# Starting the x w_val products earlier in the attention loop: two w_val tiles loaded and decoded two steps sooner, three column tiles open at once

## The chip, the core and the metric

The kernel runs on one core of a Trainium2 chip. The metric is the device time of one execution in microseconds, lower is better. Engines are named as the profile names them: PE (TensorE matmul; PEld is its weight load), DVE (VectorE), ACT (ScalarE), POOL (GpSimd), SP (the engine whose queue issues the loads).

## The reference, cut to what matters

```
for each chunk c of 32 tokens, every batch and head:                  # attention over a local window
    k_full = [mem_k (8 keys), k[c_start-16 : c_end+8]]                # the same for v
    a = softmax(q_c @ k_full.T / 8);   attn[c] = a @ v_full
x = attn as (1536 tokens, 512)
val = x @ w_val;   gate = sigmoid(x @ w_gate)                         # 512 x 1536 weights
x = (gate * val) @ w_out
out = sum over 4 experts e of  p[:, e] * (relu(x @ w1[e]) @ w2[e])    # p: normalized domain_probs
```

`w_gate`, `w_val` and `w_out` arrive as 64-bit numbers; the kernel decodes them itself.

## The kernel before

**The attention loop.** The tokens form 4 blocks of 384, the heads 4 pairs; a *unit* is one pair in one block, 16 units in all, block by block. The loop over `i` (0 to 16) runs *step* i, and in each step three units are in work: the queries and keys of unit i+1 are multiplied (`S`, 24 + 6 matmuls), the exponentials of unit i are transposed on PE (`T`), copied out on ACT (`C`), and multiplied by the values of unit i-1 (`O`), whose normalized result is transposed too (`X`). What X leaves in PSUM is split into a high part `xs` on ACT (`H`, line 1034) and a low part on DVE (`L`, line 1038): together they are rows of x, 128 columns of one block.

**The order is written by hand.** Each engine executes its instructions in the order in which the program names them. `FIRST`, `STEP0` (steps 0 to 4) and `STEP` (later steps) are strings of letters that give this order: `O{h} S{j} T{i} Q{q} R{r} a{h} r{h} N{h} m{j} M{j} s{j} W{w} C{i} F{fa} X{h} W{w2} b{t} A{t} H{h} c{t} E{j} L{h} F{fb} D{t}` with h = i-1, j = i+1. Besides those above: `a r N` are DVE's normalization, `m M s` mask, maximum and scaling of the maximum (DVE, line 972 the last), `E` the six exponentials on ACT, `Q` the loads of the unit four ahead, `R` raw weight tiles up to a number, `W` warm-up matmuls on zeros (line 933), `F` a number of products of x and w_val ("fills").

**Decoding a weight tile.** `b A c D` decode one raw tile: `b` shifts the low word (DVE, line 136), `A` rescales the high word (ACT, line 142), `c` joins them (DVE, line 146), and `D` makes the high part (ACT, line 160) and the low part (POOL, line 161). `TICKS` says in which steps this is done, `AHEAD` how many raw tiles are to be loaded by each step; the ring of raw tiles has four buffers.

**The products.** One *fill* is one product of a 128 x 128 piece of w_val with 384 tokens of x, written (f, k) below: column tile f of w_val, and rows k, which are the columns of x that unit k of the block made. It takes three matmuls: line 181 (high, high), line 182 (w high, x low) and line 183 (w low, x high). Four of them, k = 0 to 3, fill a tile in PSUM (`pv`), which ACT copies out (line 1053). The pool of these tiles has three buffers; the warm-ups write into one more tile of the same pool. `FILLS` says how many fills each step takes; up to step 3 all of them stand at the end of the step, from step 4 on half of them (`fa`) before T and X. The list `todo` gives their order.

**After the loop** PE goes on with the rest of x w_val, the gate, w_out and the experts, until the end of the span.

Of the kernel before, what the change touches and what calls it, by code (L numbers as in the profile page):

```python
# [38 lines left out]
RAWS = 4  # L39
# [13 lines left out]

VW = NG * NC * (D + 1)
KQ = VW + KC
TICKS = (0, 0, 1, 1, 1, 1, 1, 1, 1, 1, 1, 1, 1, 1)
FILLS = (0, 0, 0, 2, 3, 4, 4, 4, 4, 9, 9, 9, 9, 9, 10, 10, 10)
AHEAD = (1, 2, 3, 4, 5, 6, 7, 8, 9, 10, 11, 12)
WARM = (2, 2, 2, 2, 0)
WARM_2 = (1, 1, 1, 0, 0)  # L60

FIRST = "W10 S0 m0 M0 s0 Q3 E0 W5"
N0 = 5
STEP0 = (
    "O{h} S{j} T{i} Q{q} R{r} a{h} r{h} N{h} m{j} M{j} s{j} W{w} C{i} F{fa} X{h} W{w2} b{t} A{t} H{h} c{t} E{j} L{h} "
# [7 lines left out]
def fused_kernel(ctx: ExitStack, tc: tile.TileContext, kq0, kq1, kvw, kvc, vl, w_g, w_v, w_o, w_1, w_2, probs, out):  # L73
# [6 lines left out]
    def ps_tile(name):  # L80
        pool = banks[0]
        if banks[1] is not None:
            pool = banks[n_ps[0] % 8 >= 3]
            n_ps[0] += 1
        return pool.tile([128, 512], F32, tag="m", name=name)
# [23 lines left out]
    def raw_to(n):  # L109
        while len(raws) < min(n, n_64):  # L110
            i = len(raws)
            r = rawp.tile([128, 1024], U32, tag="raw", name=f"raw{i}")
            nc.sync.dma_start(out=r, in_=src[order[i][0]][order[i][1]].bitcast(U32))
            raws.append(r)
# [35 lines left out]
    def split_now(tp, n):  # L150

        up, down = raw_parts(n)
        t2 = low_bits(tp, n, down)
        yield
        t1 = high_bits(tp, n, up)
        yield
        joined(t1, t2)
        yield
        w = w_tile(wp, order[n])
        nc.scalar.copy(out=w[:, 0], in_=t1)  # L160
        nc.gpsimd.tensor_tensor(out=w[:, 1], in0=t1, in1=f32(w[:, 0]), op=ALU.subtract)  # L161
# [23 lines left out]
    def bt(blk):  # L185
        return slice(blk * BT, (blk + 1) * BT)
# [706 lines left out]
    with tc.tile_pool(name="gp1", bufs=NV) as gp1:  # L893
        begun = [0]
# [15 lines left out]
        def load(m):  # L910

            if m >= n_u + 2:
                return
            kv, n = kv_b[m % 3], keys(m)
            if m == 0:
                nc.sync.dma_start(out=kv[:, KQ - KB:KQ + BT + KB], in_=kq0)
                return
            for h in range(2):
                c = KQ - n if h == 0 else KQ
                if m == 1:  # L920
                    src, c1 = kq1[h], c + n + BT
                elif m < n_u:
                    src = kvw[m - 2, h] if m < N_ONCE else kvc[m - N_ONCE, h]
                    c, c1 = c - (VW if h == 0 else 0), c + n + BT + (VW if h else 0)
                else:
                    src, c = vl[m - n_u, h], c - VW if h == 0 else c + BT + n
                    c1 = c + VW
                nc.sync.dma_start(out=kv[h::2, c:c1], in_=src)

        def warm_up(n):  # L930

            for _ in range(n):
                nc.tensor.matmul(out=ps_w[:, :BT], lhsT=zero[:, :128], rhs=zero, start=True, stop=True)
# [106 lines left out]
        def proj(ps, key, t, k):  # L1040
            w, x = W[key], x_t[k]
            c = slice(k * 128, (k + 1) * 128)
            mm3(ps[:, :t.stop - t.start], w[:, 0, c], w[:, 1, c], x[:, 0, t], x[:, 1, t], k == 0, k == KD - 1)

        def v_part(blk, steps):

            pss = {}
            for f, k in steps:
                if k == 0:
                    pss[f] = ps_tile(f"pv{f}_{blk}")  # L1050
                proj(pss[f], ("v", f), bt(blk), k)
                if k == KD - 1:
                    nc.scalar.copy(out=g_t[f][:, bt(blk)], in_=pss.pop(f)[:, :BT])
                yield
# [15 lines left out]
        def g_tile(pool, f):  # L1070
            g_t[f] = pool.tile([128, B * S], F32, tag="g", name=f"g{f}")

        with tc.tile_pool(name="ps_s", bufs=2, space=PSUM) as ps_s, \
                tc.tile_pool(name="ps_t", bufs=2, space=PSUM) as ps_t, \
                tc.tile_pool(name="ps_x", bufs=1, space=PSUM) as ps_o, \
                tc.tile_pool(name="att", bufs=1) as att:
            kv_b = [att.tile([128, 2 * KQ + BT], F32, name=f"kv{i}") for i in range(3)]
            zero = att.tile([128, BT], mybir.dt.bfloat16, name="zero")
            nc.vector.memset(zero, 0.0)

            def clear(eng, i, c0, c1):
                eng.memset(kv_b[i][:, c0:c1], 0.0)

            R0, KL = KQ + BT, KC - KB
            load(0)
            clear(nc.vector, 1, KQ - KB, KQ)
            clear(nc.vector, 1, R0, R0 + KB)
            clear(nc.gpsimd, 2, KL, KQ)
            clear(nc.vector, 2, R0, R0 + KB + VW)
            load(1)  # L1090
            load(2)
            clear(nc.vector, 0, KL, KL + VW)
            clear(nc.gpsimd, 0, R0 + KB, R0 + KB + VW)
            make_identity(nc, ident)
            clear(nc.gpsimd, 1, KL, KL + VW)
            clear(nc.gpsimd, 1, R0 + KB, R0 + KB + VW)
            for i in range(3):
                clear(nc.vector, i, 0, KL)
                clear(nc.vector, i, R0 + KB + VW, R0 + KQ)
            warm = tp.tile([128, 1], F32, tag="warm", bufs=1, name="warm")  # L1100
            nc.scalar.activation(out=warm, in_=ident[:, 0:1], func=AF.Exp)
            nc.gpsimd.dma_start(out=p_in, in_=probs)
            for f in range(NV):
                g_tile(gp1, f)

            def parts(blk, fs):
                steps = [(f, k) for f in fs for k in range(KD)]
                return [v_part(blk, steps)] * len(steps)

            todo = [v_part(0, [(0, 0), (0, 1), (0, 2), (1, 0), (1, 1), (1, 2), (0, 3), (1, 3)])] * 8  # L1110
            todo += parts(0, range(2, 6)) + parts(1, range(4)) + parts(0, [6]) + parts(1, range(4, 7)) + parts(0, [7])
            todo += parts(1, [7]) + parts(2, range(NV))
            at = [0]

            def fill_to(n):
                while at[0] < min(n, len(todo)):
                    next(todo[at[0]])
                    at[0] += 1

            tk = []  # L1120
            parts_of = dict(S=scores, m=mask, M=max_, s=neg_max, E=exps, T=turn, C=turned, O=values, a=sums, r=inverse,
                            N=normal, X=put_x, H=x_hi, L=x_lo)

            def run(ops):

                for op in ops.split():
                    what, i = op[0], int(op[1:])
                    if what in parts_of:
                        if 0 <= i < n_u:
                            parts_of[what](i)  # L1130
                    elif what == "Q":
                        load(i)
                    elif what == "R":
                        raw_to(i)
                    elif what == "b" and i:
                        tk.append(split_now(tp, begun[0]))
                        begun[0] += 1
                        next(tk[0], None)
                    elif what in "Ac" and i:
                        next(tk[0], None)  # L1140
                    elif what == "D" and i:
                        next(tk.pop(), None)
                    elif what == "F":
                        fill_to(at[0] + i)
                    elif what == "W":
                        warm_up(i)

            ps_w = ps_tile("warm")
            run(FIRST)
            for i in range(n_u + 1):  # L1150
                n = FILLS[i]
                run((STEP0 if i < N0 else STEP).format(
                    h=i - 1, i=i, j=i + 1, q=i + 4, t=TICKS[i] if i < len(TICKS) else 0, fa=n // 2 if i > 3 else 0,
                    fb=n - n // 2 if i > 3 else n, r=AHEAD[i] if i < len(AHEAD) else begun[0] + RAWS - 1,
                    w=WARM[i] if i < len(WARM) else 0, w2=WARM_2[i] if i < len(WARM_2) else 0))
            fill_to(len(todo))
            for gen in todo:
                for _ in gen:
                    pass
            nc.vector.reduce_sum(out=p_sum, in_=p_in, axis=AX.X)  # L1160
            nc.vector.tensor_scalar(out=p_sum, in0=p_sum, scalar1=1e-9, scalar2=None, op0=ALU.add)
            nc.vector.reciprocal(out=p_sum, in_=p_sum)
            nc.vector.tensor_tensor(out=p_sb, in0=p_in, in1=p_sum.to_broadcast([128, NT, NE]), op=ALU.mult)
        with tc.tile_pool(name="gp2", bufs=KF - NV) as gp2, \
# [30 lines left out]
            for c in range(NCT):  # L1195
# [3 lines left out]
                for f in range(KF):  # L1199
                    i = c * KF + f  # L1200
# [119 lines left out]
```

## Time and profile before

| | us |
|---|---|
| median of 3 runs (lowest to highest) | 841.86 (841.25 to 843.28) |
| the profiled execution: its own time | 843.08 |
| the profiled execution: span of the program in the trace | 841.3 |
| PE busy in the span | 834.4 (99%) |
| DVE, ACT, POOL busy | 513.6, 392.0, 84.7 |

The profile is that of one execution. A busy PE is not a PE at its peak: matmuls are pipelined, a recorded matmul overlaps the next one, and the distance from one start to the next is what it costs.

### The profile page before, as it was taken

The numbers are of one execution on the slowest core, as the hardware profiler recorded it, in microseconds if no ns is written. First come the engines' busy times: TensorE is split into PE (matmuls) and PEld (weight loads), VectorE is DVE, ScalarE is ACT, GpSimd is POOL, SyncE is SP. The second block draws the span as 40 slices with busy tenths as digits, with TensorE's granted clock in tenths as the row PEclk, the third lists the DMA queues.
The fourth block names the chain that finished last, engine by engine and source line by source line (L and its number), as shares of the span: only waits on it lengthen the run. The fifth ranks groups of instructions, "written<-read, shape, count | busy, mean of one in ns | idle before, by whom it ended". The sixth has DMA issues, their size and how long they took to land.

```text
span 841.3 us, 13728 instructions
## 1 busy us (share of the span) xinstructions
PE 834.4 (99%) x5246; PEld 756.6 (90%) x5246; DVE 513.6 (61%) x966; ACT 392.0 (47%) x832; POOL 84.7 (10%) x98
## 2 busy tenths in 40 slices
PE   9999999999999999999999999999999999999997
PEld 6899998888888888889989989989999999999997
DVE  6754246432342229387988788788757557646747
ACT  4865355332232335435345345346355445545542
POOL 2321000000000000000000000000001343243231
PEclk9999999999999999999999999999999999999999
DMA  7976043211210001595887887731697999999983
GB/s 273 378 263 205 2 151 121 79 51 51 76 61 15 0 1 76 213 322 209 336 307 261 340 308 256 296 129 51 229 349 222 256 298 330 297 276 303 336 184 95
DMA packets 63058, 168.32 MB, mean 200 GB/s; under 512 B 6656, under 2 KB 28560, under 8 KB 62992
## 3 DMA queue, kind: packets, MB, share of 16 engines
q1 hardware_dynamic: 52160, 157.59, 52.4%
q0 software_dynamic: 10832, 9.86, 7.6%
q8 instruction: 41, 0.67, 0.3%
q14 instruction: 25, 0.20, 0.1%
HBM read 103.06 MB, written 54.53 MB: 187 GB/s over the span
## 4 chain that ended last, share of the span: by engine, by line
PE 98%; ACT 1%; DMA 0%; DVE 0%; POOL 0%; issue 0%; ACTq 0%
PE b L181 5%; PE d L182 5%; PE d L183 5%; PE b L182 5%; PE b L183 5%; PE d L181 5%; PE pv L181 4%; PE pv L183 4%; PE pv L182 4%; PE pg L182 4%; PE pb L182 4%; PE pb L181 4%; PE pg L183 4%; PE pg L181 4%; PE pb L183 4%; PE B L183 3%
## 5 line engine op out<-in xcount | busy, mean ns | idle before, releaser
L530 POOL DMA_DIRECT2D acc<-st x57 | 49.3, 950 | 673.7 <-DVE st L528 673.2
L181 PE MATMUL b<-yo,w 128*128 128x384 f32 x256 | 87.3, 341 | 0.7 <-ACT s L766 0.7
L182 PE MATMUL b<-yo,w 128*128 128x384 f32 x256 | 86.4, 337 | 0.0
L183 PE MATMUL b<-yo,w 128*128 128x384 f32 x256 | 86.3, 337 | 0.0
L766 ACT COPY s<-b 128x384 f32<-128x384 f32 x64 | 30.7, 479 | 95.9 <-PE b L183 95.7
L181 PE MATMUL pv<-xs,w_v 128*128 128x384 f32 (+1 forms) x176 | 64.2, 365 | 0.0
L183 PE MATMUL pv<-xs,w_v 128*128 128x384 f32 (+1 forms) x176 | 61.8, 351 | 0.3 <-POOL w_v L161 0.3
L182 PE MATMUL pv<-xs,w_v 128*128 128x384 f32 (+1 forms) x176 | 61.5, 349 | 0.0
L1062 ACT ACTIVATE sg<-pg 128x512 f32<-128x512 f32 x36 | 21.5, 598 | 84.2 <-PE pg L183 84.2
L183 PE MATMUL pg<-xs,w_g 128*128 128x512 f32 x144 | 56.0, 389 | 0.0
L182 PE MATMUL pg<-xs,w_g 128*128 128x512 f32 x144 | 56.0, 389 | 0.0
L181 PE MATMUL pb<-hl,w_o 128*128 128x512 f32 x144 | 56.0, 389 | 0.0
L182 PE MATMUL pb<-hl,w_o 128*128 128x512 f32 x144 | 56.0, 389 | 0.0
L183 PE MATMUL pb<-hl,w_o 128*128 128x512 f32 x144 | 56.0, 389 | 0.0
L181 PE MATMUL pg<-xs,w_g 128*128 128x512 f32 x144 | 56.0, 389 | 0.0
L120 DVE TENSOR_TENSOR hl<-g,hl 128x512 fp32r<-128x512 f32 x36 | 24.7, 690 | 48.5 <-ACT hl L119 48.5
L181 PEld LDWEIGHTS b<-yo,w 128*128 128x128 f32 x256 | 48.1, 188 | 3.9 <-ACT s L766 2.8
L182 PEld LDWEIGHTS b<-yo,w 128*128 128x128 f32 x256 | 48.1, 188 | 1.0
L183 PEld LDWEIGHTS b<-yo,w 128*128 128x128 f32 x256 | 48.1, 188 | 0.0
L119 ACT CAST hl<-g 128x512 fp32r<-128x512 f32 x36 | 22.2, 623 | 54.8 <-PE pb L183 54.8
L181 PE MATMUL e<-yo,w 128*128 128x384 f32 x128 | 43.2, 338 | 0.0
L182 PE MATMUL e<-yo,w 128*128 128x384 f32 x128 | 43.1, 337 | 0.0
(759 smaller groups left out, 2290.7 us busy)
## 6 DMA issues: line engine op xcount, KB each, us to landing
kept<-w SPq DMA_DIRECT2D x77, 512.0 KB, 4.8
w<-kept SPq DMA_DIRECT2D x49, 512.0 KB, 10.0
w_ring<-kept SPq DMA_DIRECT2D x38, 512.0 KB, 7.5
raw<-in_w_dram SPq DMA_DIRECT2D x34, 512.0 KB, 6.2
kept<-w SPq DMA_DIRECT2D x42, 256.0 KB, 7.2
kv<-in_kvc_dram SPq DMA_DIRECT2D x20, 483.0 KB, 6.1
acc<-st POOLq DMA_DIRECT2D x75, 128.0 KB, 5.5
raw<-in_w_v_dram SPq DMA_DIRECT2D x12, 512.0 KB, 6.2
```

Of the source, the lines that this page charges most:

```text
L119: nc.scalar.copy(out=hi, in_=src)
L120: nc.vector.tensor_tensor(out=lo, in0=src, in1=f32(hi), op=ALU.subtract)
L181: nc.tensor.matmul(out=ps, lhsT=w_hi, rhs=r_hi, start=first, stop=False, skip_group_check=more)
L182: nc.tensor.matmul(out=ps, lhsT=w_hi, rhs=r_lo, start=False, stop=False, skip_group_check=more)
L183: nc.tensor.matmul(out=ps, lhsT=w_lo, rhs=r_hi, start=False, stop=last, skip_group_check=more)
L530: nc.gpsimd.dma_start(out=a, in_=st, accum_op=ALU.add)
L766: nc.scalar.copy(out=s, in_=ps[:, :HT])
L1062: nc.scalar.activation(out=sg, in_=ps, func=AF.Sigmoid)
```

## The change

The raw tiles 0 and 1 of w_val are asked for before the loop (`R2` in `FIRST`), the later ones two steps sooner, and decoding goes through steps 0 to 11 instead of 2 to 13. The fills of steps 0 to 16 go from 0 0 0 2 3 4 4 4 4 9 9 9 9 9 10 10 10 to 0 1 3 4 4 4 4 4 4 9 9 9 9 9 8 8 7: 96 in both, and the seven that steps 1 to 4 gain are those that steps 14 to 16 lose. The first fills go through three column tiles together: in step 1 (0,0); in step 2 (0,1), (1,0), (1,1); in step 3 (0,2), (1,2), (2,0), (2,1); in step 4 (2,2), (0,3), (1,3), (2,3). All fills of step 4 now stand at its end too. By the two lists the warm-ups inside the loop go from 11 to 7, four fewer (the change's own description says six).

```
-TICKS = (0, 0, 1, 1, 1, 1, 1, 1, 1, 1, 1, 1, 1, 1)
-FILLS = (0, 0, 0, 2, 3, 4, 4, 4, 4, 9, 9, 9, 9, 9, 10, 10, 10)
-AHEAD = (1, 2, 3, 4, 5, 6, 7, 8, 9, 10, 11, 12)
-WARM = (2, 2, 2, 2, 0)
-WARM_2 = (1, 1, 1, 0, 0)
-
-FIRST = "W10 S0 m0 M0 s0 Q3 E0 W5"
+TICKS = (1, 1, 1, 1, 1, 1, 1, 1, 1, 1, 1, 1)
+FILLS = (0, 1, 3, 4, 4, 4, 4, 4, 4, 9, 9, 9, 9, 9, 8, 8, 7)
+AHEAD = (3, 4, 5, 6, 7, 8, 9, 10, 11, 12)
+WARM = (2, 2, 1, 0, 0)
+WARM_2 = (1, 1, 0, 0, 0)
+
+FIRST = "W10 S0 m0 M0 s0 R2 Q3 E0 W5"
...
-            todo = [v_part(0, [(0, 0), (0, 1), (0, 2), (1, 0), (1, 1), (1, 2), (0, 3), (1, 3)])] * 8
-            todo += parts(0, range(2, 6)) + parts(1, range(4)) + parts(0, [6]) + parts(1, range(4, 7)) + parts(0, [7])
+            todo = [v_part(0, [
+                (0, 0), (0, 1), (1, 0), (1, 1), (0, 2), (1, 2), (2, 0), (2, 1), (2, 2), (0, 3), (1, 3), (2, 3)])] * 12
+            todo += parts(0, range(3, 6)) + parts(1, range(4)) + parts(0, [6]) + parts(1, range(4, 7)) + parts(0, [7])
...
-                    h=i - 1, i=i, j=i + 1, q=i + 4, t=TICKS[i] if i < len(TICKS) else 0, fa=n // 2 if i > 3 else 0,
-                    fb=n - n // 2 if i > 3 else n, r=AHEAD[i] if i < len(AHEAD) else begun[0] + RAWS - 1,
+                    h=i - 1, i=i, j=i + 1, q=i + 4, t=TICKS[i] if i < len(TICKS) else 0, fa=n // 2 if i > 4 else 0,
+                    fb=n - n // 2 if i > 4 else n, r=AHEAD[i] if i < len(AHEAD) else begun[0] + RAWS - 1,
```

On PE, step 2 of the kernel before: the values of unit 1 (o1), the scores of unit 3, the transposes of unit 2 and of x of unit 1 (x1), and then at once the values of unit 2 (o2). LDWEIGHTS and MATMUL of L933 on zeros are warm-ups.

```order
L1003 MATMUL o1_299<-kv0_110,at1_282 32x130 x12
L951 MATMUL s3_312<-kv0_110 32x2x56 x12
L953 MATMUL s3_312<-kv0_110 128x2x8 x3
L987 MATMUL t2_328<-ident_72,a2_291 128x128 x3
L933 LDWEIGHTS zero_113
L933 MATMUL warm_149<-zero_113 128x384
L933 LDWEIGHTS zero_113
L933 MATMUL warm_149<-zero_113 128x384
L1026 MATMUL x1_349<-ident_72,xn1_339 128x128 x3
L933 LDWEIGHTS zero_113
L933 MATMUL warm_149<-zero_113 128x384
L1003 MATMUL o2_372<-kv1_111,at2_347 32x130 x12
```

The same step on PE in the changed kernel, from the transposes of unit 2 on: xs1 is the split of x1 that ACT and DVE make after x1.

```order
L987 MATMUL t2_352<-ident_72,a2_308 128x128 x3
L933 LDWEIGHTS zero_113
L933 MATMUL warm_149<-zero_113 128x384
L1026 MATMUL x1_372<-ident_72,xn1_363 128x128 x3
L181 MATMUL pv0_0_316<-xs1_376,w_v_0_243 128x384
L182 MATMUL pv0_0_316<-xs1_376,w_v_0_243 128x384
L183 MATMUL pv0_0_316<-xs1_376,w_v_0_243 128x384
L181 MATMUL pv1_0_394<-xs0_300,w_v_1_320 128x384
L182 MATMUL pv1_0_394<-xs0_300,w_v_1_320 128x384
L183 MATMUL pv1_0_394<-xs0_300,w_v_1_320 128x384
L181 MATMUL pv1_0_394<-xs1_376,w_v_1_320 128x384
L182 MATMUL pv1_0_394<-xs1_376,w_v_1_320 128x384
```

Two warm-ups are gone, and between x1 and o2 stand three fills, of which the first reads xs1.

On DVE, the same step of the changed kernel: the mask of unit 3's scores, their maximum and its scaling, the shift of raw tile 2 (L136), its joining (L146) and the low part of x1.

```order
L960 MEMSET s3_336 32x2x16
L967 TENSOR_REDUCE nm3_366<-s3_336 128x6
L972 TENSOR_SCALAR nm3_366<-nm3_366 128x6
L136 TENSOR_SCALAR t2_2_377<-raw2_220 128x512
L146 SCALAR_TENSOR_TENSOR t1_2_379<-t1_2_379,t2_2_377 128x512
L1038 TENSOR_TENSOR xs1_376<-x1_372,xs1_376 128x384
```

The order within the step is that of before (there with raw tile 0); in steps 0 and 1, which had no decoding, L136 and L146 are new.

On the SP queue, the difference at its start: raw tiles 0 and 1 now stand ahead of the second load into kv0.

```order
 L928 DMA kv2_112<-in_kvw_dram 64x1580 x2
+L113 DMA raw0_180<-in_w_v_dram 128x1024
+L113 DMA raw1_182<-in_w_v_dram 128x1024
 L928 DMA kv0_110<-in_kvw_dram 64x1580 x2
 L928 DMA kv1_111<-in_kvw_dram 64x1580 x2
-L113 DMA raw0_216<-in_w_v_dram 128x1024
+L113 DMA raw2_220<-in_w_v_dram 128x1024
 L928 DMA kv2_112<-in_kvw_dram 64x1580 x2
```

After that each step issues its unit's loads and then one raw tile, as before, the raw tile being two further on.

## Rows read from the trace of the kernel before

**Rows 1.** The page, chain that ended last: shares of the span by engine.
```profile
PE 98%; ACT 1%; DMA 0%; DVE 0%; POOL 0%; issue 0%; ACTq 0%
```
**Rows 2.** Waits of PE, 20 to 120 us; busy times of the stretch 23 to 45 us.
```profile
PE pv L183 <- POOL w_v L161: 0.3, 1, 0.3
...
23.00:45.00 22.00, 22.00 (x334) 19.58 (x333) 16.84 (x46) 17.09 (x54) 6.43 (x5) 1.00 0.98 374
```
**Rows 3.** Timeline, step 2: start us, us, engine, line, operation [idle before <-releaser].
```profile
17.26 0.53 PE L987 MATMUL t<-ident,a 128*128 128x128 f32 x3
...
17.62 0.49 PE L933 MATMUL warm<-zero 128*128 128x384 bf16 x2
...
17.82 0.48 ACT L994 COPY at<-t 128x384 f32<-128x384 f32 x1 [0.96 <-PE t L987]
17.95 0.49 PE L1026 MATMUL x<-ident,xn 128*128 128x128 f32 x3
...
18.20 0.69 ACT L142 ACTIVATE t<-raw 128x512 f32<-128x512 f32 x1
18.28 0.33 PE L933 MATMUL warm<-zero 128*128 128x384 bf16 x1
...
18.93 0.69 DVE L146 SCALAR_TENSOR_TENSOR t<-t,t 128x512 uint32<-128x512 uint32 x1 [0.23 <-ACT t L142]
...
19.54 0.55 DVE L1038 TENSOR_TENSOR xs<-x,xs 128x384 fp32r<-128x384 f32 x1
```
**Rows 4.** Timeline, step 3, and the start of step 5.
```profile
20.60 0.53 PE L987 MATMUL t<-ident,a 128*128 128x128 f32 x3
...
21.09 1.28 POOL L161 TENSOR_TENSOR w_v<-t,w_v 128x512 fp32r<-128x512 f32 x1 [16.02 <-ACT w_v L160]
...
21.75 0.65 DVE L972 TENSOR_SCALAR nm<-nm 128x6 f32<-128x6 f32 x1
...
22.43 0.44 PE L183 MATMUL pv<-xs,w_v 128*128 128x384 f32 x1 [0.29 <-POOL w_v L161]
...
22.88 0.34 PE L182 MATMUL pv<-xs,w_v 128*128 128x384 f32 x1
...
23.32 0.87 PE L1003 MATMUL o<-kv,at 128*32 128x130 f32 x24
23.44 0.55 DVE L1038 TENSOR_TENSOR xs<-x,xs 128x384 fp32r<-128x384 f32 x1
...
27.76 0.87 PE L1003 MATMUL o<-kv,at 128*32 128x130 f32 x24
```
**Rows 5.** Timeline, steps 0 and 1, and the first matmuls of step 2.
```profile
11.90 1.34 ACT L979 ACTIVATE a<-s,nm 128x64 f32<-128x64 f32 x6
...
13.93 0.53 PE L987 MATMUL t<-ident,a 128*128 128x128 f32 x3
...
14.94 0.17 DVE L972 TENSOR_SCALAR nm<-nm 128x6 f32<-128x6 f32 x1
...
15.20 0.87 PE L1003 MATMUL o<-kv,at 128*32 128x130 f32 x24
```
**Rows 6.** Timeline, step 8.
```profile
48.60 0.33 PE L181 MATMUL pv<-xs,w_v 128*128 128x384 f32 x1
...
49.12 0.49 PE L987 MATMUL t<-ident,a 128*128 128x128 f32 x3
...
50.48 0.34 PE L182 MATMUL pv<-xs,w_v 128*128 128x384 f32 x1
...
50.54 0.56 DVE L1038 TENSOR_TENSOR xs<-x,xs 128x384 fp32r<-128x384 f32 x1 [1.17 <-ACT xs L1034]
```
**Rows 7.** SP's second issue of loads; loads 0 to 40 us: KB, median us to landing.
```profile
2.76 1.23 SPq L928 DMA_DIRECT2D kv<-in_kvw_dram  x2
...
raw<-in_w_v_dram SPq DMA_DIRECT2D x8, 512.0 KB, 6.6
```
**Rows 8.** Timeline, the ten warm-ups at the start.
```profile
1.13 3.38 PE L933 MATMUL warm<-zero 128*128 128x384 bf16 x10 [1.13 <-DVE zero L1079]
```

## The prediction

> **What bounds the kernel now.** I read the page's chain first: PE is 98% of what ended last [rows 1], so what PE loses anywhere in front, without a later slack to take it up, is lost at the end. Then the waits of the loop: from 20 to 120 us PE waits once for another engine, 0.29 us for the low part of the first w_val tile, and never for a load, although the DMA engines are 98% busy from 23 to 45 us [rows 2]. So the loop is a dense PE row in which other engines' latencies are hidden, in its first steps partly by warm-ups. Then the timeline of the first steps, to see what stands ready when. The reader is to see in step 2 [rows 3] how late the low part of x is. T2 starts at 17.26. ACT copies it at 17.82, and only then, in its order, rescales the raw tile (18.20). DVE joins that tile at 18.93, and only then, in its order, makes the low part of x1, from 19.54 to 20.09: 2.83 us after T2's start. The transpose x1 itself was over on PE at 18.28. Before, nothing on PE asks for xs1 until two steps later; what follows x1 is a warm-up and o2.
>
> **The change, part by part.** A fill that reads the x of its own step now stands right behind that step's X: (0,0) in step 1, (0,1) in step 2, (0,2) in step 3, and (0,3), behind one other fill, in step 4. Its second matmul (L182) reads the low part. PE is in order, so o of the next step, and behind it S and T, wait too; and since ACT's copy needs T, the chain to the next low part begins only after that. I walk the four steps with these durations:
>
> - from o's start to T's start, 2.06 us (15.20 to 17.26) [rows 3, 5];
> - from T's start to the end of the low part, 2.83 us with a decoding in the step [rows 3];
> - from that end to L182's start 0.06, as from POOL's end at 22.37 to L183 at 22.43; from an L182 of a step's last fill to the next o 0.44 (22.88 to 23.32) [rows 4]. Together 0.50;
> - each further fill 0.52 us (48.60 to 49.12) [rows 6].
>
> In step 1 one thing is not as in step 2. POOL's part of tile 0 is now made there: the exponentials of unit 1 (11.90 to 13.24) move back by a 0.69 us rescaling, ACT's high copy follows, and POOL then runs from about 14.3 to 15.6, where DVE's scaling of the maximum comes up at 14.94 [rows 3, 5]. In step 3 of before the same meeting is in the trace: the scaling at 21.75 takes 0.65 us, to POOL's end (21.09 + 1.28), where it takes 0.17 us at 14.94, and the low part of that step ends at 23.99, 3.39 us after T3 [rows 4, 5]. For step 1 I take 3.39, nearest by its situation; the lower bound is 2.83. The Trainium skill, page "SBUF — State Buffer", section "SBUF: two separate sides", says that a VectorE operation in a two-port mode and a GpSimd operation take the shared pair of ports as an exclusive lock for a whole instruction; by that rule the sum is the 6.9 us below, and without the meeting it would be 6.4.
>
> The walk, in us of the trace. Step 1: T1 at 13.93 as before, low part at 17.32, o1 at 17.82. Step 2: T2 at 19.88, low part 22.71, two more fills behind: o2 at 24.25. Step 3: T3 26.31, low part 29.14, three more: o3 at 31.20. Step 4: T4 33.26; X3 and the fill (2,2) take about 1.2 us from there and lie inside the wait; low part 36.09, two more: o4 at 37.63. Before, o4 began at 27.76 [rows 4], so step 5 begins 9.87 us later. By then PE has done 12 fills instead of 5. The seven others are taken from steps 14 to 16, which are PE's own time, and give back 7 x 0.52 = 3.64. The loss is **6.2 us**. In the walk the four warm-ups that go (0.165 each, two between 17.62 and 17.95 [rows 3]; 0.66 together) and the 0.29 us wait for POOL are already left out.
>
> A fifth wait stands in step 8. Before, its fills were of block 0. By the new counts they are (0,0) to (0,3) of block 1, and (0,3) reads the x of unit 7, made in that step, with one fill between. In step 8 of before the second fill behind X has its L182 at 50.48, and the low part ends at 51.10 [rows 6]: L182 would start at 51.16, **0.7 us** later. No decoding stands in front of the low part there, because `STEP` puts it ahead of T. Blocks 2 and 3 are begun a step or more behind their x, in both kernels.
>
> At no cost I put these. *The loads*: raw tile 0 is issued behind the loads that SP issues from 2.76 to 3.99, and with the median landing of 6.6 us it is there at about 10.6 [rows 7]; ACT wants it just ahead of unit 1's exponentials, at about 11.9 [rows 5]. If it came later than that, all from T1 on moves; I allow up to 0.5 us for it. The loads of keys behind it on SP's queue are asked for no earlier than their buffers come free, and the longer steps give them more time. *Decoding two steps sooner*: ACT has C, A, H, E and D in step 2 of before, and that step is 3.34 us long, from T2 to T3 (17.26 to 20.60) [rows 3, 4]; the steps are now 5 us and more. *The third open tile*: its bank is that of the warm-ups, which are over by then in PE's own order; tile 3 needs tile 0 copied out, some 2 us before.
>
> Sum: 6.2 + 0.7 = 6.9 us. The profiled execution took 843.08 around a span of 841.3; its like would be a span of 848.2 and 850.0. That execution lies 1.2 above the median, so the median becomes 841.86 + 6.9 = **848.8**. Bounds of the known terms: without the meeting in step 1 (-0.6), without the 0.06 lags (-0.3) and step 8's wait (-0.7), 847.2; with raw tile 0 late, 849.3.
>
> **Rivals.** *The loads set the pace, and the lateness costs nothing.* The DMA engines are 98% busy from 23 to 45 us; if each unit's keys came just before S, PE would wait for them anyway, and the raw loads moved into the start would even help. Then only the warm-ups and the wait count: 841.86 - 0.66 - 0.29 = 840.9. It decides if S in steps 5 to 9 waits for keys for 7 us in sum, and against it stands that PE waits for no load in that stretch [rows 2]. A smaller form, in which some later slack takes up about half, gives 845.4; the chain at 98% PE [rows 1] leaves little room.
>
> *PE's clock falls back.* The ten first warm-ups take 0.34 us each [rows 8], the later ones 0.165 [rows 3]: 384 columns at 1.2 and at 2.4 GHz, though the granted clock of the page reads full in both places. Now warm-ups go, and PE stands still for about 1.8 us (x1's end to L182) in each of four steps. If one step fell to the lower level, its 2.06 + 0.44 + 1.04 = 3.5 us of PE work would take twice as long: 3.5 more, 852.3; all of steps 2 to 4, some 859. For it speaks that PE began at the lower level after standing still; against it that over half of each of these steps is still PE work. The Trainium skill, page "TensorE: Matmul & The Clock Gate", section "Part 1: The HAM clock gate", says that throttled is the default and activity releases it, so that pauses between bursts can bring the half rate back; no run here has shown a fall in mid-kernel.
>
> *Not what it says*: four warm-ups go instead of six; the two would have been worth 0.3 us, nothing beside the rest.
>
> **How the numbers follow.** The forecast 0.80; the clock 0.10; the half taken up 0.05; the loads 0.05. About 0.3% (2.5 us) is what a measurement of this kernel can tell from no change. The loads' case at 840.9 is "same"; I leave 0.03 for "faster", which no mechanism in the trace gives, since all that PE can save in the loop's start is the warm-ups and 0.29 us. Same 0.07, slower 0.90. The range goes from the half case (845.4) to one step of lower clock (852.3).
>
> **What would show it.** In the profile after, PE waits of L182 `pv` for DVE `xs` L1038, four between 15 and 36 us, the largest 1.5 to 2 us, and one of about 0.6 near 60 us; o4 at about 37.6; then the same step lengths as before and steps 14 to 16 shorter by 1.0 to 1.6 us. ACT's wait for raw tile 0 would show the loads late; L951 groups of 24 at 1.3 us in place of 0.76 would show the clock. The prediction is wrong if the low part of x ends less than half a microsecond behind X, or if step 5 and those behind it run shorter than before.

## The result, and the profile after

The changed kernel is slower: a median of 851.31 us in 5 runs (850.89 to 852.30) against 843.28 us in 5 runs of the kernel before (841.25 to 846.52), a ratio of 1.0099 (95% interval 1.0072 to 1.0125; the ratios here are formed over all runs and are not those of the two medians). On a second chip, among the experiments below, it was 851.91 against 841.61, 1.0122 (1.0108 to 1.0136). The forecast was 848.8, within 845.4 to 852.3. The profiled execution took 850.89 us around a span of 848.9, 7.6 us more than the span before.

The page's chain that ended last, for the changed kernel, and under it PE's waits from 10 to 130 us (us in total, times, longest):

```profile
PE 97%; DVE 1%; ACT 1%; DMA 0%; issue 0%; ACTq 0%; DVEq 0%
```
```profile
PE pv L181 <- ACT xs L1034: 3.5, 4, 1.2
PE pv L182 <- DVE xs L1038: 2.1, 5, 0.8
```

PE, 98% of that chain before [rows 1], has given a per cent to DVE, and where it waited once, for POOL [rows 2], it now waits nine times for x: four times for the high part from ACT and five times for the low part from DVE. Step 2 of the changed kernel, from the timeline (start us, us, engine, line, operation, idle before and its releaser), beside [rows 3]:

```profile
20.03 0.52 PE L987 MATMUL t<-ident,a 128*128 128x128 f32 x3
...
20.55 0.49 PE L1026 MATMUL x<-ident,xn 128*128 128x128 f32 x3
20.59 0.48 ACT L994 COPY at<-t 128x384 f32<-128x384 f32 x1 [2.69 <-PE t L987]
20.96 0.67 ACT L142 ACTIVATE t<-raw 128x512 f32<-128x512 f32 x1
21.53 0.46 ACT L1034 CAST xs<-x 128x384 fp32r<-128x384 f32 x1
21.66 0.69 DVE L146 SCALAR_TENSOR_TENSOR t<-t,t 128x512 uint32<-128x512 uint32 x1 [0.20 <-ACT t L142]
22.05 0.44 PE L181 MATMUL pv<-xs,w_v 128*128 128x384 f32 x1 [1.01 <-ACT xs L1034]
22.27 0.55 DVE L1038 TENSOR_TENSOR xs<-x,xs 128x384 fp32r<-128x384 f32 x1
22.88 0.44 PE L182 MATMUL pv<-xs,w_v 128*128 128x384 f32 x1 [0.39 <-DVE xs L1038]
...
24.49 0.87 PE L1003 MATMUL o<-kv,at 128*32 128x130 f32 x24
```

x1 follows T2 behind one warm-up. ACT copies T2 out, rescales the raw tile, and only then makes the high part (21.53); DVE joins the tile and only then makes the low part, 2.79 us after T2's start. L181 waits for the one, L182 for the other, and o2 stands behind both and two further fills. Now step 1's end and step 8:

```profile
14.17 0.53 PE L987 MATMUL t<-ident,a 128*128 128x128 f32 x3
...
14.47 1.27 POOL L161 TENSOR_TENSOR w_v<-t,w_v 128x512 fp32r<-128x512 f32 x1 [9.39 <-ACT w_v L160]
...
15.10 0.66 DVE L972 TENSOR_SCALAR nm<-nm 128x6 f32<-128x6 f32 x1
...
16.80 0.55 DVE L1038 TENSOR_TENSOR xs<-x,xs 128x384 fp32r<-128x384 f32 x1
...
17.41 0.45 PE L182 MATMUL pv<-xs,w_v 128*128 128x384 f32 x1 [0.77 <-DVE xs L1038]
...
38.03 0.87 PE L1003 MATMUL o<-kv,at 128*32 128x130 f32 x24
...
53.93 0.49 PE L987 MATMUL t<-ident,a 128*128 128x128 f32 x3
...
55.35 0.56 DVE L1038 TENSOR_TENSOR xs<-x,xs 128x384 fp32r<-128x384 f32 x1
...
55.96 0.44 PE L182 MATMUL pv<-xs,w_v 128*128 128x384 f32 x1 [0.15 <-DVE xs L1038]
...
56.51 0.87 PE L1003 MATMUL o<-kv,at 128*32 128x130 f32 x24
```

In step 1 the meeting of DVE's scaling with POOL is there: 0.66 us, to POOL's end at 15.74 within 0.02 us, as in [rows 4]. o4 begins at 38.03, 10.27 us later than before [rows 4].

**A ledger for the runs below.** The rest of this document compares executions by o0 (the start of step 1's PE work) and o8 (the start of step 9's). The time from o0 to o8, less 0.52 us for each fill that a kernel has done by then beyond the 21 of before, less 33.59 us (45.45 - 11.86, before), is what the loop's first steps cost more than before. For the changed kernel it is 44.41 - 7 x 0.52 - 33.59 = 7.2 us. The lines it uses, o0 and o8 before, then o0 after (o8 after, at 56.51, is shown above):

```profile
11.86 0.87 PE L1003 MATMUL o<-kv,at 128*32 128x130 f32 x24
45.45 0.87 PE L1003 MATMUL o<-kv,at 128*32 128x130 f32 x24
```
```profile
12.10 0.87 PE L1003 MATMUL o<-kv,at 128*32 128x130 f32 x24
```

### The profile page after: what moved, and what is told of

It reads as the page before. It is cut to its first block, busy times and chain, and to the rows that moved or that the text cites. A ratio compares the mean times of both kernels' runs of the same rounds, so it can differ in the third digit from the quotient of the medians.

```text
span 848.9 us, 13714 instructions
## 1 busy us (share of the span) xinstructions
PE 836.5 (99%) x5242; PEld 756.3 (89%) x5242; DVE 513.5 (60%) x966; ACT 391.7 (46%) x832; POOL 84.7 (10%) x98
## 4 chain that ended last, share of the span: by engine, by line
PE 97%; DVE 1%; ACT 1%; DMA 0%; issue 0%; ACTq 0%; DVEq 0%
PE b L181 5%; PE d L183 5%; PE b L182 5%; PE d L182 5%; PE b L183 5%; PE d L181 5%; PE pv L181 4%; PE pv L182 4%; PE pv L183 4%; PE pg L183 4%; PE pb L183 4%; PE pb L182 4%; PE pg L181 4%; PE pg L182 4%; PE pb L181 4%; PE B L183 3%
## 5 line engine op out<-in xcount | busy, mean ns | idle before, releaser
L181 PE MATMUL b<-yo,w 128*128 128x384 f32 x256 | 87.4, 341 | 0.7 <-ACT s L766 0.7
L182 PE MATMUL b<-yo,w 128*128 128x384 f32 x256 | 86.4, 338 | 0.0
L181 PE MATMUL pv<-xs,w_v 128*128 128x384 f32 (+1 forms) x176 | 64.6, 367 | 3.6 <-ACT xs L1034 3.5
L182 PE MATMUL pv<-xs,w_v 128*128 128x384 f32 (+1 forms) x176 | 62.0, 352 | 2.1 <-DVE xs L1038 2.1
L182 PE MATMUL pg<-xs,w_g 128*128 128x512 f32 x144 | 56.0, 389 | 0.0
L181 PE MATMUL pb<-hl,w_o 128*128 128x512 f32 x144 | 56.0, 389 | 0.0
L182 PE MATMUL pb<-hl,w_o 128*128 128x512 f32 x144 | 56.0, 389 | 0.0
L181 PE MATMUL pg<-xs,w_g 128*128 128x512 f32 x144 | 56.0, 389 | 0.0
L181 PEld LDWEIGHTS b<-yo,w 128*128 128x128 f32 x256 | 48.1, 188 | 4.1 <-ACT s L766 3.0
L182 PEld LDWEIGHTS b<-yo,w 128*128 128x128 f32 x256 | 48.1, 188 | 1.0
L181 PE MATMUL e<-yo,w 128*128 128x384 f32 x128 | 43.2, 338 | 0.0
L182 PE MATMUL e<-yo,w 128*128 128x384 f32 x128 | 43.1, 337 | 0.0
```

Of the source, the lines that this page charges most:

```text
L181: nc.tensor.matmul(out=ps, lhsT=w_hi, rhs=r_hi, start=first, stop=False, skip_group_check=more)
L182: nc.tensor.matmul(out=ps, lhsT=w_hi, rhs=r_lo, start=False, stop=False, skip_group_check=more)
```

## The experiments

Every kernel was compared with the kernel before on its own chip; the first four share 21 runs of it (median 841.52), the next four other 21 (841.61).

| run | median us (runs) | ratio to before, 95% interval | o0, o8 of the profiled execution | span | ledger us |
|---|---|---|---|---|---|
| decode_only | 842.74 (11) | 1.0013 (1.0004 to 1.0021) | 12.10, 45.54 | 841.5 | -0.2 |
| lag | 842.05 (11) | 1.0004 (0.9994 to 1.0013) | 12.01, 46.89 | 840.8 | -0.8 |
| warm_back | 851.34 (5) | 1.0114 (1.0097 to 1.0130) | 9.78, 60.18 | 852.6 | 13.2 |
| low_first | 846.78 (5) | 1.0063 (1.0051 to 1.0076) | 9.98, 52.34 | 844.7 | 5.1 |
| after_again | 851.91 (4) | 1.0122 (1.0108 to 1.0136) | 9.63, 57.02 | 849.4 | 10.2 |
| warm_fill | 849.63 (4) | 1.0098 (1.0084 to 1.0112) | 9.61, 55.26 | 847.6 | 8.4 |
| decode_step1 | 841.94 (11) | 1.0004 (0.9995 to 1.0013) | 12.11, 45.57 | 841.4 | -0.1 |
| lag_step1 | 841.11 (11) | 1.0001 (0.9991 to 1.0011) | 10.01, 44.70 | 839.1 | -0.5 |

The theory: PE waits in steps 1 to 4 and 8 for the x of the same step. The rivals: the early decoding itself, the raw loads put ahead of the keys, the third open tile, the clock with fewer warm-ups.

**decode_only**: the early half of the change, without the fills.

```
-TICKS = (0, 0, 1, 1, 1, 1, 1, 1, 1, 1, 1, 1, 1, 1)
+TICKS = (1, 1, 1, 1, 1, 1, 1, 1, 1, 1, 1, 1)
-AHEAD = (1, 2, 3, 4, 5, 6, 7, 8, 9, 10, 11, 12)
+AHEAD = (3, 4, 5, 6, 7, 8, 9, 10, 11, 12)
-FIRST = "W10 S0 m0 M0 s0 Q3 E0 W5"
+FIRST = "W10 S0 m0 M0 s0 R2 Q3 E0 W5"
```

> The kernel before with only the early loads and the early decoding (raw tiles 0 and 1 ahead of the loop, decoding in steps 0 to 11); fills, their order and the warm-ups as before. If the loss of about 8 us is the fills' wait for the low part of x, this costs nothing: within 1 us of the kernel before, o4 at about 27.8 in the trace, and the 0.29 us wait for POOL gone. If the loss comes from decoding in steps 0 and 1 on ACT and DVE, or from the raw loads ahead of the keys, most of it shows here: 4 to 8 us slower, with ACT or PE waiting for raw tiles or keys.

In the trace o4 begins at 27.85 and PE waits for no other engine; 7 us are not here. But the medians show 1.2 us, a little over the 1 us allowed: a small real loss that neither side had named, and the trace shows none of it. It stays open until decode_step1.

**lag**: the changed kernel with fills that lag a step behind their x.

```
-FILLS = (0, 1, 3, 4, 4, 4, ..., 8, 8, 7)
+FILLS = (0, 0, 2, 4, 3, 4, ..., 9, 9, 8)
-(0, 0), (0, 1), (1, 0), (1, 1), (0, 2), (1, 2), (2, 0), (2, 1), (2, 2), (0, 3), (1, 3), (2, 3)
+(0, 0), (1, 0), (0, 1), (1, 1), (2, 0), (2, 1), (0, 2), (1, 2), (2, 2), (0, 3), (1, 3), (2, 3)
```

> The changed kernel (early loads and decoding, three open column tiles, its seven warm-ups) with fills that never read the x of their own step: two in step 2 (x of unit 0), four in step 3 (units 0 and 1), three in step 4 (units 0 to 2), from then on four and nine. If the wait for the low part is the cause, PE has no wait on xs, and the time is that of the kernel before or up to 1.2 us less (four warm-ups and the POOL wait). If three open tiles, fewer warm-ups or early decoding are the cause, it stays 4 to 8 us slower.

PE's only wait from 10 to 130 us is now this one:

```profile
PE x L1026 <- DVE s L960: 0.2, 1, 0.2
```

With early decoding, three open tiles and seven warm-ups as in the changed kernel, the loss of 8 to 10 us is gone: 0.5 us over before by the medians, within the measurement. So it is which x the fills read and when, and none of those three.

**low_first**: the changed kernel, with x's split ahead of the decoding in `STEP0`.

```
-... F{fa} X{h} W{w2} b{t} A{t} H{h} c{t} E{j} L{h} F{fb} D{t}
+... F{fa} X{h} W{w2} H{h} L{h} b{t} A{t} c{t} E{j} F{fb} D{t}
```

> The changed kernel with one reordering in steps 0 to 4: ACT's high part and DVE's low part of x stand ahead of the decoding of the raw tile instead of behind its rescaling and joining. The low part should end about 2.0 us after T's start instead of 2.8 (as in step 8, where no decoding stands in front), in all four steps: 3.4 to 3.7 us come back of about 8, and each wait of PE shrinks to about 1 us. If the order of x and decoding on ACT and DVE does not set the wait, the time stays that of the changed kernel.

Its step 2 in the timeline:

```profile
18.08 0.52 PE L987 MATMUL t<-ident,a 128*128 128x128 f32 x3
...
19.13 0.48 ACT L1034 CAST xs<-x 128x384 fp32r<-128x384 f32 x1
...
19.50 0.67 ACT L142 ACTIVATE t<-raw 128x512 f32<-128x512 f32 x1
19.64 0.56 DVE L1038 TENSOR_TENSOR xs<-x,xs 128x384 fp32r<-128x384 f32 x1 [0.45 <-ACT xs L1034]
...
20.25 0.45 PE L182 MATMUL pv<-xs,w_v 128*128 128x384 f32 x1
```

The low part ends 2.12 us after T2's start, where the changed kernel had 2.79. By the ledger 5.1 us are lost, against the 8.4 of warm_fill, whose steps begin as early (o0 at 9.61) and whose clock stays up: 3.3 us back, just under the 3.4 to 3.7 that the theory gave, 0.7 to 1.0 us in each of steps 1 to 4. So that part of the loss comes from the decoding that ACT and DVE have ahead of the split; the 5.1 us that stay do not.

**warm_back**: the changed kernel with the 11 warm-ups of before (`WARM = (2, 2, 2, 2, 0)`, `WARM_2 = (1, 1, 1, 0, 0)`).

> The changed kernel with the four warm-ups put back (11 in the loop, as before). If PE only waits for the low part, they lie inside that wait, and the time is that of the changed kernel within 0.5 us (ratio to before 1.009 to 1.010). If the loss came from a PE clock that fewer warm-ups let fall, several us come back.

The median, 851.34, is the changed kernel's, as the theory said, though the ratio, 1.0114, is above the one expected. But the profiled execution was the longest of the five (854.63), and its clock did fall: the mean granted clock was 0.991, and 0.50 from 16 to 28 us, that is 1.2 GHz (PE busy, granted clock, DMA share and GB/s of that stretch):

```profile
16.00:28.00 12.00, 11.51 (x90) 0.50 0.65 236
```

The execution whose mean granted clock was 1.000 took 849.46 us. So the clock rival was not wrong in kind, only that these four warm-ups do not hold it off. That led to the next two.

**after_again**: the changed kernel as it is.

> The changed kernel itself once more, beside the others on one chip. Expected: 8 to 10 us over the kernel before. Open is why it is more than the 7.4 us that the two profiles show up to step 9. Theory: in executions in which PE reaches its full clock before the scores of unit 1 (near 6 us instead of 10), ACT reaches the rescaling of raw tile 0 before the tile has landed (a wait of 1.1 to 1.3 us), and PE's clock falls to the lower level after the waits. Then some of its executions have a mean granted clock under 0.999. Rival: the rest is scatter between chips, and clocks are like those of before.

Waits of ACT from 5 to 16 us; then stretches with PE busy, granted clock (here 0.52, 0.63 and 1.00), DMA share and GB/s; then the timeline of step 2's first fill:

```profile
ACT t L142 <- DMA raw<-in_w_v_dram: 1.4, 1, 1.4
```
```profile
20.00:22.00 2.00, 0.61 (x3) 1.00 0.80 213
22.00:24.00 2.00, 2.00 (x7) 0.52 1.01 362
24.00:26.00 2.00, 2.00 (x43) 0.63 0.50 199
26.00:28.00 2.00, 1.92 (x32) 1.00 0.00 0
```
```profile
19.55 0.49 PE L1026 MATMUL x<-ident,xn 128*128 128x128 f32 x3
21.04 0.44 PE L181 MATMUL pv<-xs,w_v 128*128 128x384 f32 x1 [1.01 <-ACT xs L1034]
21.87 0.53 PE L182 MATMUL pv<-xs,w_v 128*128 128x384 f32 x1 [0.39 <-DVE xs L1038]
22.20 0.53 PE L183 MATMUL pv<-xs,w_v 128*128 128x384 f32 x1
22.52 0.53 PE L181 MATMUL pv<-xs,w_v 128*128 128x384 f32 x1
```

Both parts of the theory are in this one execution. PE's step 0 ran at full clock, ACT came to raw tile 0 early and waited 1.4 us for it. And after the waits of steps 1 and 2 the clock fell: fills follow each other at 0.32 us a matmul from 22.20 on, 1.2 GHz, where the first profile of the changed kernel has 0.18. The nine executions of the changed kernel had mean granted clocks of 0.995 to 0.999, five of them under 0.998; the kernel before had 0.998 to 1.000 on the two chips of these runs. The loss by the medians, 10.3 us, is a little over the 8 to 10 expected. The expectation's 7.4 us up to step 9 is the ledger's 7.2 with the 0.24 by which o0 itself came later.

**warm_fill**: warm-ups into the waits themselves, `WARM_2 = (1, 7, 7, 8, 0)` instead of `(1, 1, 0, 0, 0)`: by the lists six, seven and eight more in steps 1 to 3.

> The changed kernel with warm-ups filled into the waits: 7 more behind X in step 1, 7 in step 2 and 8 in step 3 (step 4 can't have any there, its third column tile has taken their bank). They take 0.165 us each and lie inside waits of 1.2 us or more, so the waits for the low part stay and no useful work moves. If the clock falls in the waits are part of the loss, all executions now have a mean granted clock of 0.998 or more, and 1 to 3 us of the changed kernel's loss come back; if the clock plays no part, the time is that of the changed kernel within 0.5 us.

The same stretch, and step 2 in the timeline:

```profile
20.00:26.00 6.00, 5.62 (x76) 1.00 0.74 254
```
```profile
19.24 0.49 PE L1026 MATMUL x<-ident,xn 128*128 128x128 f32 x3
19.57 1.30 PE L933 MATMUL warm<-zero 128*128 128x384 bf16 x7
20.77 0.44 PE L181 MATMUL pv<-xs,w_v 128*128 128x384 f32 x1
21.59 0.44 PE L182 MATMUL pv<-xs,w_v 128*128 128x384 f32 x1 [0.38 <-DVE xs L1038]
21.87 0.33 PE L183 MATMUL pv<-xs,w_v 128*128 128x384 f32 x1
```

The wait for the low part is as long as ever, L182 starts as long after x1 as without the warm-ups (2.35 us against 2.32), but the clock stays at 2.4 GHz, and the kernel with 21 more matmuls is 2.3 us faster than the changed kernel beside it (849.61 to 850.21 us against 850.84 to 852.63). By the ledger after_again's execution lost 10.2 - 8.4 = 1.8 us more: 0.3 in step 1, where the raw tile came 0.3 us later, and about 1.5 in steps 2 and 3, which is what the fall cost there.

**decode_step1**: the kernel before with the early loads, and decoding one step sooner instead of two (`TICKS = (0, 1, 1, ...)`, `AHEAD = (2, 3, 4, ...)`).

> The kernel before with early loads, but decoding from step 1 on (one step sooner than before, instead of two). Decoding from step 0 on cost 1.2 us by the medians. If that was ACT's wait for raw tile 0 in step 0, it is gone here: within 0.4 us of the kernel before. If it was ACT's and DVE's extra work in the first steps or the place of the loads in the queue, about 1 us stays.

842.74 - 841.52 = 1.2 us have become 0.3, within the expectation: the loss of decode_only was in step 0, where ACT stands in front of raw tile 0. decode_only's profiled execution shows no wait there, since its PE came late to step 1 (o0 at 12.10); after_again's and warm_fill's, with o0 near 9.6, do (1.4 and 1.1 us). That it is this wait that costs decode_only its 1.2 us is therefore inferred. The spans agree with it: decode_only's shortest is 840.2 us where the kernel before has 839.1, while the longest are 841.7 and 842.2, so only executions with an early PE lose.

**lag_step1**: lag, with decoding from step 1 on and `FILLS = (0, 0, 1, 3, 4, 4, ...)`.

> Fills that never read the x of their own step, decoding from step 1 on, seven warm-ups, three open column tiles: one fill in step 2, three in step 3, four from step 4 on. No wait of PE on xs and no wait of ACT for raw tile 0. Expected 0.5 to 1.1 us below the kernel before (four warm-ups and the wait for POOL); 0.5 us above it, as with decoding from step 0 on, if the raw tile's wait was not what was left there.

The median is 0.5 us below that of before, the ratio over all runs 1.0001 (0.9991 to 1.0011): no difference that can be told. The ledger of its profiled execution says -0.5. What the change could have won, four warm-ups and the POOL wait (of which 0.2 us stay here), is about that, and a measurement of this kernel does not resolve it.

**before_again, before_look2, before_look3**: the kernel before, three single executions, to have one whose PE is at full clock early (by the length of the second scores, since the granted clock reads 1.00 in both cases).

> The kernel before, one more profiled execution. In most of its executions the span is near 839.5 us, 2 us under the one profiled first. Theory: in those PE reaches its full clock before the scores of unit 1, o0 begins near 9.6 us instead of 11.9, and everything behind is as in the first profile (o8 33.6 us behind o0), without a wait for a raw tile in step 0, where nothing is decoded. Rival: the 2 us lie somewhere else, and o0 begins near 11.9.

> The kernel before once more, since its last profiled execution had a span of 841.8 us and o0 at 11.9. If this one has a span near 839.5, o0 should begin near 9.6 us and o8 33.6 us later; with a span near 841.5 it tells nothing new.

> The same kernel and the same expectation, for a second chance of an execution with a span near 839.5 us.

Spans 841.8, 841.8 and 839.1; only the last was of the kind looked for. From the first profile of before, the second scores of the program; then the same and o8 from before_look3:

```profile
8.84 1.30 PE L951 MATMUL s<-kv 128*32 128x112 f32 x24
```
```profile
6.97 0.78 PE L951 MATMUL s<-kv 128*32 128x112 f32 x24
```
```profile
43.21 0.87 PE L1003 MATMUL o<-kv,at 128*32 128x130 f32 x24
```

Those scores take 0.78 us at 6.97; in the first profile of before they took 1.30 at 8.84. o0 is at 9.61 and o8 33.60 behind it, as in the first profile (33.59). So 2.2 us between executions of one kernel are PE's clock rising before unit 1's scores or behind them. before_look2 was a third thing: o0 at 10.23, then a wait of 2.0 us for raw tile 0 in step 2 and 0.7 us of PE for a load of keys and values. So in the kernel before too, that tile can come late.

## Why the prediction was right

*The wait for the low part*, worked out as 6.2 us, is shown by lag (gone with the order of the fills), low_first (shorter with the order of the split) and the nine waits in the profile. The sign that the prediction named came in another shape: not four waits of L182 with the largest at 1.5 to 2 us, but waits of L181 for ACT's high part, up to 1.2 us, which it had not named, and behind them waits of L182 of up to 0.8. The low part still ends last, so the sum does not change. The walk gave o1 to o4 at 17.82, 24.25, 31.20 and 37.63; they are at 17.96, 24.49, 31.52 and 38.03. 0.24 us of the last difference is already there at T1 (14.17 instead of 13.93). The meeting with POOL in step 1 was there; the low part came 3.18 us after T1, between the two bounds of 2.83 and 3.39. (Without the meeting the sum is 6.9 - 0.56 = 6.3, not the prediction's 6.4.)

*The give-back* held: o8 is 11.06 us later than before, and the span 7.6, that is 3.5 returned for seven fills priced at 3.64. Steps 9 to 13 together keep their length (35.17 us before, 35.16 after), and steps 14 and 15 are 1.0 us shorter each, as forecast.

*Step 8's wait* held: the step takes 5.21 us (51.30 to 56.51), before 4.43 (41.02 to 45.45), 0.8 instead of the 0.7. But the prediction read it off the wrong step. What stands in [rows 6] is step 9, whose T is at 49.12; step 8's T is at 43.65. There L182 of the second fill behind X is at 45.01 and the low part ends at 45.63, the same 0.6 us apart, so the term came out by a slip that did no harm.

*Raw tile 0* is the term that was mis-sized. The prediction put it at no cost with up to 0.5 us allowed, because ACT would want the tile at about 11.9 and it would land at 10.6. The 11.9 came from one execution in which PE was at the lower clock until about 10 us. In four profiled executions with an early PE (after_again, warm_fill, warm_back, low_first) ACT is there at 9.6 to 9.9 and starts on the tile at 10.7 to 11.2: it waits 1.1 to 1.4 us, and the loss is 8.4 instead of 7.2 us by the ledgers of warm_fill and the first profile, 1.2 us, all of it in step 1 (o0 to o1 takes 7.04 us instead of 5.86). It is chance that the first profile of the changed kernel, too, is of an execution with a late PE, so that its 7.2 us come so near the sum of 6.9.

*The clock* was given as a rival with one chance in ten and 3.5 us for a step. It happens: in part of the executions, for part of a step or more, about 1.5 us in after_again and some 5 us in warm_back's profiled one (13.2 - 8.4). There the whole of step 2 ran at a granted clock of 0.50 and took 10.05 us (o1 to o2), 3.5 more than the 6.55 in warm_fill: the rival's price for one step came out. So the loss of 10.3 us on the second chip is the forecast's mechanism with raw tile 0 added to it and, by warm_fill, about two microseconds of this rival on top. The 8.0 of the first comparison is less mainly because of the kernel before: three of its five runs there took over 843 us, on the second chip 4 of 21, while the medians of the changed kernel are only 0.6 us apart. The measured 851.31 us lie above the 849.3 that the prediction's known terms allowed, and within its range only because that went on to 852.3 for the clock.

The prediction's sentence on the Trainium skill, page "TensorE: Matmul & The Clock Gate", section "Part 1: The HAM clock gate", that pauses between bursts can bring the half rate back, ended with no run showing a fall in mid-kernel; after_again and warm_back now show one. That the loads set the pace, or that later slack takes the lateness up, is out: in the profile after PE waits for no load from 10 to 130 us, and the 7.4 us left of the lateness at o8 after seven fills are still there at the end (7.6).

## What to carry to other kernels

An engine that executes in order waits where the first use of a late operand stands, so before work is moved forward, read from the trace when its last operand is made, including what stands ahead of the maker in its own queue; here L182 starts 1.8 to 2.1 us after the end of X, four times. Warm-ups put into waits that were there anyway cost nothing (21 more in warm_fill, and 2.3 us less), while useful work moved to a place where its operand is late cost 8 to 10 us. And before a landing time is set against the time at which a transfer is wanted, take that second time from more than one execution: here it varied by 2 us with nothing changed.

## What was not expected of the hardware

The granted clock of the profile read 1.00 from the start in every kernel, though the first warm-ups took 0.34 us each [rows 8], twice the later ones; in the fall in mid-kernel it read 0.50 to 0.52, with the same doubled matmuls. And in after_again PE fell back after a stretch in which it had stood still only in pieces, the longest idle pieces being 0.67, 1.21 and 1.01 us by its waits, with a whole O, S and T (2.07 us of work) between the second and the third; in warm_back it had fallen by the end of the second of two, 0.67 and 1.20 us.
